# Four-piece GpSimd squares and low halves in chunks 0 and 1, ScalarE casts for half of w_out, and later joins for the last quarter-row of w_in

## The chip, the cores and the metric

One core of a Trainium2 chip runs the whole problem. The metric is the device time of one launch in microseconds, lower is better. TensorE (PE) multiplies, VectorE (DVE), ScalarE (ACT) and GpSimd (POOL) do the elementwise work, SyncE (SP) issues the DMAs. TensorE's clock has two levels, 1.2 and 2.4 GHz; the granted clock is shown as a share of the higher one.

## The reference, cut to what matters

```python
# attention, 8 batches, 8 heads, 512 local and 32 global tokens, head size 64
s_g = scale * q_g @ k_all^T              # global queries see all 544 keys
s_l = [scale * q_l @ k_g^T, scale * q_l @ k_l^T where |i - j| <= 32]
attn_out = concat(softmax(s_g) @ v_all, softmax(s_l) @ v_all)
# feed-forward on the 8 * 544 = 4352 tokens
x = attn_out as (8 * 544, 512)
h = x @ w_in                             # w_in 512 x 2048, in double precision
g = h * cos(h)
out = (g @ w_out).astype(float32)        # w_out 2048 x 512, in double precision
```

## The kernel before

**Numbers.** The two weights arrive as 64-bit doubles. ScalarE scales the upper word (`decode`, L231), VectorE shifts the lower word (L232) and joins the two into one float32 (L236, the "join"). A float32 is then carried as two float16 halves: a high half by a cast (`split_w`, L243) and a low half, value minus high half, by GpSimd (`pool_tt`, L217). x and g get the same split: `xh`/`xl` (L669 ScalarE, L670 VectorE) and `gh`/`gl` (L849 ScalarE, L850 GpSimd). Each product is three float16 matmuls: high by high, high by low, low by high.

**w_in** comes in eight pieces (row quarter kc = k // 2, column half k % 2): `w_in_load`, `w_in_max`, `w_in_piece`. Pieces 4 and 7 come as two halves of 512 columns (`raw_wi7_0`, `raw_wi7_1`). **w_out** comes in 16 pieces of 128 rows (`w_out_load`, `w_out_max`, `w_out_piece`); their largest values are reduced at L250 into `wos`, for pieces 8 to 15 from a first copy, `raw_wm8` to `raw_wm15`, which is loaded again later as `raw_wo8` to `raw_wo15` for the decoding.

**The stages.** Up to about 82 us the attention of batch 0 and w_in's preparation run. From there feed-forward chunks follow, two of 256 tokens per batch and one for the global tokens, each in eight steps j of two column blocks of h:

- `m1_a`: h into PSUM tile `ph_c_j` (L805, 24 matmuls of 256 columns; three buffers of `ph`)
- `m1_b`: `u` by ScalarE (L827) and VectorE (L828)
- `m1_c`: `w` = sine by ScalarE (L429)
- `m1_d`: the square of `w` on GpSimd (L843), `gf` on VectorE (L845, the last reader of `ph_c_j`, which frees its buffer), `gh` on ScalarE (L849), `gl` on GpSimd (L850)
- `m2_a`: two output tiles `po` (L865, 12 matmuls of 512 columns), which needs both w_out pieces 2j and 2j + 1

Beside chunks 0 and 1 run w_out's 16 pieces and the whole attention of batch 1 (scores `ps` L531, masked minimum `t` L549, exponentials L429, normalised `planes` L596/L597, DMA transposes `pt` L616, values `acc` L649, global queries `gacc` L741). Later chunks run beside the next batch's attention alone. `chunk_scales` prepares the chunk's constants `ca`, `cm`, `co`.

**Order.** Work is written down with `at(slot, phase, f, ...)`; `pr` gives the priority. A scheduler then places each engine's instructions, and a queue runs in that order: an instruction that waits holds everything behind it. `behind(ins, what)` orders an instruction after another one. The SP queue is one row too: a load that waits for its buffer holds the transposes behind it.

The few lines that matter most:

```python
WH = "DDDDDDDDDDDDDDDD"          # engine of w_out's 16 casts: all VectorE
SPLIT = 256                      # pool_tt: pieces of at most this many columns
decode(z, raw, wfs["s", kc], join_after="xs" if k >= 6 else "dx" if k >= 4 else None)
split_w(wo_h[:, j], wo_l[:, j], z, j % 4 < WLV, WH[j])
nc.gpsimd.tensor_tensor(w, w, w, op=ALU.mult)               # m1_d
nc.gpsimd.tensor_tensor(gl, gf, gh, op=ALU.subtract)        # m1_d
```

Of the kernel before, what the change touches and what calls it, by code (L numbers as in the profile page):

```python
# [15 lines left out]
ALU = mybir.AluOpType  # L16
# [30 lines left out]
SPLIT = 256  # L47
# [19 lines left out]
TPE = [1, 1, 1, 1]  # L67
TPV = [1, 0, 1, 0]
WLV = 0
MR = 2  # L70
SR = (1,)
AR = (1,)
WH = "DDDDDDDDDDDDDDDD"
DI = 3
QMA = 1
KQB = 3
# [15 lines left out]
W0 = -15  # L92
WE = -20
WM = 1
WL = [-22, -20, -17]
# [27 lines left out]
def body(tc, qf, v, wi, wo, mask, out):  # L123
    nc = tc.nc
# [4 lines left out]
    with ExitStack() as ctx:  # L129
# [11 lines left out]
        msk = cp.tile([P, MW], BF16, name="msk")  # L141
# [67 lines left out]
        def pool_tt(o, a, b, op, n=SPLIT):  # L209

            w = o.shape[-1]
            k = -(-w // n)
            while w % k:
                k += 1
            for i in range(k):
                c = slice(i * (w // k), (i + 1) * (w // k))
                nc.gpsimd.tensor_tensor(o[..., c], a[..., c], b[..., c], op=op)  # L217
# [21 lines left out]
            )  # L239
            behind(join.ins, join_after)  # L240

        def split_w(h, l, z, on_vector=False, cast="A"):
            {"A": nc.scalar.copy, "D": nc.vector.tensor_copy, "G": nc.gpsimd.tensor_copy}[cast](h, z)  # L243
            if on_vector:
                nc.vector.tensor_tensor(l, z, h, op=ALU.subtract)
            else:
                pool_tt(l, z, h, ALU.subtract)

        def raw_max(o, raw):
            return nc.vector.tensor_reduce(  # L250
# [28 lines left out]
        wfs = {}  # L279
# [45 lines left out]
        def w_in_piece(k):  # L325
            kc = k // 2
            parts = wfs.pop(("raw", k))
            n = 1024 // len(parts)
            for a, raw in enumerate(parts):
                c = slice(k % 2 * 1024 + a * n, k % 2 * 1024 + a * n + n)  # L330
                z = raw.bitcast(F32)[:, 1::2]
                decode(z, raw, wfs["s", kc], join_after="xs" if k >= 6 else "dx" if k >= 4 else None)
                split_w(wi_h[:, kc, c], wi_l[:, kc, c], z)

        wfi = cp.tile([P, 2], F32, name="wfi")
# [65 lines left out]
        def w_out_piece(j):  # L401
            if j < 8:
                raw = wo_raw[:, j]
            else:
                raw = w2.tile([P, 1024], U32, tag="raw", name=f"raw_wo{j}")
                nc.sync.dma_start(raw.bitcast(I64), wo[j * P : (j + 1) * P])
            z = w2.tile([P, DM], F32, tag="wy", name=f"z_wo{j}")
            decode(z, raw, wsc, low_after="wsc")
            split_w(wo_h[:, j], wo_l[:, j], z, j % 4 < WLV, WH[j])

        def w_out_done():
            m = ap_.tile([P, 1], F32, tag="wm", name="wm_o")
# [247 lines left out]
        def av_b(b, p):  # L660
            if p == 0:
                st["x", b] = (
                    ap_.tile([P, NPAIR, SL], F16, tag="xh", name=f"xh_{b}"),
                    ap_.tile([P, NPAIR, SL], F16, tag="xl", name=f"xl_{b}"),
                )
            xh, xl = st["x", b]
            acc = st.pop(("acc", b, p))
            sx = xs[:, p : p + 1]
            hi = nc.scalar.activation(xh[:, p], acc, AF.Identity, scale=sx)  # L669
            lo = nc.vector.scalar_tensor_tensor(  # L670
                xl[:, p], acc, sx, xh[:, p], op0=ALU.mult, op1=ALU.subtract
            )
            st["last_x", b, p] = (hi.ins, lo.ins)
            st["new_x"] = hi.ins


# [161 lines left out]
        def m1_d(c, j):  # L838
            w = st.pop(("u", c, j))[1]
            n = w.shape[-1]  # L840
            gh = mp.tile([P, n], F16, tag="gh", name=f"gh_{c}_{j}", bufs=4)
            gl = mp.tile([P, n], F16, tag="gl", name=f"gl_{c}_{j}", bufs=4)
            nc.gpsimd.tensor_tensor(w, w, w, op=ALU.mult)  # L843
            gf = gf_tile(c, j, n)
            nc.vector.scalar_tensor_tensor(  # L845
                gf, w, 0.5, st.pop(("ph", c, j)).rearrange("p a b -> p (a b)"),
                op0=ALU.subtract, op1=ALU.mult,
            )
            nc.scalar.copy(gh, gf)  # L849
            nc.gpsimd.tensor_tensor(gl, gf, gh, op=ALU.subtract)  # L850
            st["g2", c, j] = (gh, gl)

        def m2_a(c, j):
# [43 lines left out]
        def at(slot, phase, f, *a, pr=None):  # L897
            e = (phase, len(ev[slot]), f, a)
            ev[slot].append(e)
            pr = (slot, phase) if pr is None else pr if isinstance(pr, tuple) else (pr, phase)  # L900
            rank[slot, e[1]] = pr + (slot, e[1])
# [1 line left out]
        rank = {}  # L903

        def attn_pair(b, p, o):
            at(o["load"], PJ, load_qk, b, p)
            attn_rest(b, p, o)

        def attn_rest(b, p, o):
# [34 lines left out]
            )  # L944


        at(-24, PA, nc.sync.dma_start, msk, mask)
        for p in range(NPAIR):
            o = tight(U0 + SP0 * p, VD0 + SP0 * p)
            o["load"] = -23 if p < 2 else -22  # L950
            if p == 3:
                o["gd"], o["ge"] = -10, -9
            attn_pair(0, p, o)
        at(-23, PJ, load_v, 0)
        at(-19, PF, v_a, 0)
        at(-19, PG, v_b, 0)
        at(-19, PG2, v_c, 0)
        for k in range(8):
            if k < 4:
                at(WL[0] if k < 2 else WL[1], PJ, w_in_load, k)  # L960
            at(WE + k - WM, PH2, w_in_max, k, pr=W0 + k - WM)
            at(WE + k if k < 4 else -13 if k < 6 else -11, PK, w_in_piece, k, pr=(W0 + k, PJ))
            if k < 4:
                at(WE + k, PJ, w_in_load, k + 4, pr=W0 + k if k < 3 else W0 - 1)
        at(WE + 7 - WM, PI, w_in_max_done, pr=(W0 + 7 - WM, PH2))
# [125 lines left out]
```

## Time and profile before

| | |
|---|---|
| median of 3 runs | 959.17 us (958.49 to 959.61) |
| the profiled execution | 958.73 us, its span 956.9 us |
| PE busy | 904.6 us (95%) |
| ACT busy | 656.2 us (69%) |
| DVE busy | 587.8 us (61%) |
| POOL busy | 401.5 us (42%) |

The busy times are means over stages with different limits. Up to 82 us no matmul of the feed-forward can run; from 82 to about 206 us chunks 0 and 1 share the engines with w_out's preparation and batch 1's attention; from 206 us on the matmuls follow one another. A view by stretches shows which engine is full where, the waits show what ended PE's idle time, and groups of instructions by form show the price of one.

### The profile page before, as it was taken

The page shows a single profiled execution, that of the slowest core. Times are in us where ns is not written, and L with a number is a line of the kernel's source. Part 1 is how long each engine was busy: PE and PEld are TensorE (multiplying, and loading weights), DVE is VectorE, ACT ScalarE, POOL GpSimd, SP SyncE. Part 2 cuts the span into 40 slices and gives each one's busy share as a digit, 9 for nine tenths or more (in the row PEclk, how much of TensorE's full clock was granted, in tenths as well). Part 3 has the DMA queues.
Part 4 walks back from the last instruction along what each step waited for, and adds up shares of the span by engine and source line. Part 5 has one row for each costly group of instructions (what it writes and reads, how often), then busy time and mean ns, then how long its engine had stood idle before and what let it go on. Part 6 is the DMA issues. An engine that isn't in the chain of part 4 may idle for free.

```text
span 956.9 us, 19857 instructions
## 1 busy us (share of the span) xinstructions
PE 904.6 (95%) x7643; PEld 602.3 (63%) x7643; DVE 587.8 (61%) x1576; ACT 656.2 (69%) x1411; POOL 401.5 (42%) x412
## 2 busy tenths in 40 slices
PE   6657988999999999999999999999999999999995
PEld 4445665556666666666666666666666666666663
DVE  5998999856474757566665757564756555423231
ACT  6886599866777677776877777677777775443341
POOL 5856555432434343433334333324343434444441
PEclk8657899999999999999999999999999999999999
DMA  9936237535244453536262724352442433000000
GB/s 365 388 126 198 69 84 179 141 70 159 53 93 86 121 111 67 111 90 144 46 133 45 186 41 124 44 151 53 108 71 67 85 67 59 23 1 23 1 23 23
DMA packets 155176, 96.41 MB, mean 101 GB/s; under 512 B 141000, under 2 KB 141128, under 8 KB 153288
## 3 DMA queue, kind: packets, MB, share of 16 engines
q1 hardware_dynamic: 155080, 95.13, 39.7%
q8 instruction: 60, 0.98, 0.4%
q14 instruction: 36, 0.29, 0.1%
HBM read 51.59 MB, written 8.91 MB: 63 GB/s over the span
## 4 chain that ended last, share of the span: by engine, by line
PE 80%; DVE 9%; ACT 3%; DMA 3%; issue 2%; POOL 2%; SPq 0%; ACTq 0%; POOLq 0%; DVEq 0%
PE ph L805 35%; PE po L865 34%; PE ps L531 5%; PE acc L649 3%; DVE planes L597 2%; PE gps L686 1%; PE gacc L741 1%; DMA raw_wo<-wo 1%; DMA vr<-v 1%; ACT t L429 1%; DVE t L549 1%; DVE raw_wi L236 1%; DVE vl L516 1%; DVE z_wo L236 1%; DMA ptg<-planes_g 1%
## 5 line engine op out<-in xcount | busy, mean ns | idle before, releaser
L865 PE MATMUL po<-wo_hl,gh 128*128 128x512 f16 x1088 | 321.3, 380 | 0.7 <-POOL wo_hl L217 0.6
L805 PE MATMUL ph<-xh,wi_h 128*128 128x256 f16 x1024 | 282.3, 276 | 3.4 <-DVE gf L845 3.4
L805 PE MATMUL ph<-xl,wi_h 128*128 128x256 f16 x1024 | 281.3, 275 | 2.1 <-DVE xl L670 2.1
L805 PE MATMUL ph<-xh,wi_l 128*128 128x256 f16 x1024 | 281.3, 275 | 0.0
L850 POOL TENSOR_TENSOR gl<-gf,gh 128x512 f16<-128x512 f32 x136 | 163.5, 1203 | 237.1 <-ACT gh L849 237.0
L843 POOL TENSOR_TENSOR w<-w 128x512 f32<-128x512 f32 x136 | 143.9, 1058 | 258.5 <-ACT w L429 249.5
L805 PEld LDWEIGHTS <-wi_h 128*128 128x128 f16 x2176 | 207.1, 99 | 57.9 <-issue 22.2
L865 PE MATMUL po<-wo_hl,gl 128*128 128x512 f16 x544 | 201.3, 380 | 0.0
L865 PEld LDWEIGHTS <-gh 128*128 128x128 f16 x1088 | 106.7, 98 | 102.3 <-issue 1.1
L849 ACT CAST gh<-gf 128x512 f16<-128x512 f32 x136 | 83.1, 613 | 126.8 <-DVE gf L845 126.8
L828 DVE SCALAR_TENSOR_TENSOR u<-u,cm,ph 128x512 f32<-128x512 f32 x136 | 101.2, 744 | 99.5 <-ACT u L827 99.5
L429 ACT ACTIVATE w<-u,ca 128x512 f32<-128x512 f32 x136 | 97.9, 721 | 93.9 <-DVE u L828 91.9
L845 DVE SCALAR_TENSOR_TENSOR gf<-w,ph 128x512 f32<-128x512 f32 x136 | 93.0, 684 | 108.7 <-POOL w L843 107.9
L429 ACT ACTIVATE t<-t,mn 128x192 f32<-128x192 f32 (+1 forms) x256 | 116.7, 458 | 10.3 <-DVE mn L549 9.8
L805 PEld LDWEIGHTS <-wi_l 128*128 128x128 f16 x1088 | 107.2, 99 | 16.7 <-issue 3.4
L597 DVE SCALAR_TENSOR_TENSOR planes<-t,sm,planes 128x192 f16<-128x192 f32 (+1 forms) x232 | 104.9, 511 | 11.7 <-ACT planes L596 10.9
L827 ACT ACTIVATE u<-ph,cm 128x512 f32<-128x512 f32 x136 | 92.0, 678 | 21.9 <-PE ph L805 15.4
L865 PEld LDWEIGHTS <-gl 128*128 128x128 f16 x544 | 53.3, 98 | 64.5 <-issue 2.1
L549 DVE CUSTOM_DVE_ANT_0 t<-ps,msk 128x192 f32<-128x192 f32 (+1 forms) x256 | 82.9, 366 | 11.7 <-PE ps L531 10.8
L596 ACT ACTIVATE planes<-t,sm 128x192 f16<-128x192 f32 (+1 forms) x232 | 86.2, 455 | 2.4 <-DVE gsm L713 2.2
L531 PE MATMUL ps<-qkr 64*128 64x192 f32 (+1 forms) x496 | 78.0, 383 | 8.4 <-DMA qkr<-qf 5.5
L429 ACT ACT_TABLE_LOAD x58 | 74.4, 1283 | 3.6 <-DVE u L828 2.0
(148 smaller groups left out, 924.5 us busy)
## 6 DMA issues: line engine op xcount, KB each, us to landing
qkr<-qf SPq DMA_DIRECT2D x31, 608.0 KB, 5.0
vr<-v SPq DMA_DIRECT2D x8, 1280.0 KB, 6.4
out<-o SPq DMA_DIRECT2D x34, 256.0 KB, 2.0
raw_wi<-wi SPq DMA_DIRECT2D x6, 1024.0 KB, 12.2
wo_hl<-wo SPq DMA_DIRECT2D x8, 512.0 KB, 11.7
raw_wm<-wo SPq DMA_DIRECT2D x8, 512.0 KB, 4.3
raw_wo<-wo SPq DMA_DIRECT2D x8, 512.0 KB, 4.7
raw_wi<-wi SPq DMA_DIRECT2D x4, 512.0 KB, 12.4
```

The lines of the kernel that those rows point to most:

```text
L429: ins = nc.scalar.activation(*a, **k).ins
L531: nc.tensor.matmul(pt[h][:, c], q[r, QZ[j] : QZ[j] + P], k[r, z : z + w], start=True, stop=True, skip_group_check=True,)
L549: nc.vector.tensor_tensor_reduce(t[:, h], pt[h], msk[:, MOFF[i] : MOFF[i] + w], NAL, 3.0e38, ALU.add, ALU.min, mn[:, h : h + 1],)
L596: a = nc.scalar.activation(hi, t[:, h], AF.Identity, scale=r)
L597: d = nc.vector.scalar_tensor_tensor(lo, t[:, h], r, hi, op0=ALU.mult, op1=ALU.subtract)
L805: nc.tensor.matmul(ph[:, a], w[:, kc, f], x[:, kc, q], start=first and ip == 0, stop=last and ip == 2, skip_group_check=True,)
L827: nc.scalar.activation(u, ph, AF.Identity, bias=m)
L828: nc.vector.scalar_tensor_tensor(u, u, m, ph, op0=ALU.subtract, op1=ALU.subtract)
L843: nc.gpsimd.tensor_tensor(w, w, w, op=ALU.mult)
L845: nc.vector.scalar_tensor_tensor(gf, w, 0.5, st.pop(("ph", c, j)).rearrange("p a b -> p (a b)"), op0=ALU.subtract, op1=ALU.mult,)
L850: nc.gpsimd.tensor_tensor(gl, gf, gh, op=ALU.subtract)
L865: nc.tensor.matmul(po[k], g[:, a * CT + k * P : a * CT + (k + 1) * P], w[:, 2 * j + a], start=(j == 0 and i == 0), stop=(j == NS - 1 and i ...
```

## The change

Five things are edited.

1. The squares (L843) and `gl` (L850) of chunks 0 and 1 go through `pool_tt` in pieces of `PS` = 128 columns: four GpSimd instructions of 128 columns in place of one of 512, 32 times. Later chunks keep one.
2. `WH`: the casts of w_out's pieces 0 to 7 move from VectorE to ScalarE.
3. `J7`, `L7`: the two joins of w_in's piece 7 are ordered behind `xl` of batch 0's last pair ("xl3"), and the piece is written down at slot -5 in place of -11.
4. `SW` = 256 is named as the width of w_out's low-half pieces, the same as `SPLIT` was.
5. `LO` writes the first loads (mask, q and k of batch 0, v of batch 0, w_in's pieces 0 and 1) as one string. The SP queue's first 31 rows stay the same.

```diff
+SW = 256
+LO = "m01v2345"
+J7 = "xl3"
+L7 = -5
+PS = 128
-WH = "DDDDDDDDDDDDDDDD"
+WH = "AAAAAAAADDDDDDDD"
...
-        def split_w(h, l, z, on_vector=False, cast="A"):
+        def split_w(h, l, z, on_vector=False, cast="A", n=SPLIT):
...
-                pool_tt(l, z, h, ALU.subtract)
+                pool_tt(l, z, h, ALU.subtract, n)
...
-                decode(z, raw, wfs["s", kc], join_after="xs" if k >= 6 else "dx" if k >= 4 else None)
+                decode(z, raw, wfs["s", kc], join_after=J7 if k == 7 else "xs" if k == 6 else "dx" if k >= 4 else None)
...
-            split_w(wo_h[:, j], wo_l[:, j], z, j % 4 < WLV, WH[j])
+            split_w(wo_h[:, j], wo_l[:, j], z, j % 4 < WLV, WH[j], SW)
...
+            if (b, p) == (0, 3):
+                st["xh3"], st["xl3"] = hi.ins, lo.ins
...
-            nc.gpsimd.tensor_tensor(w, w, w, op=ALU.mult)
+            pool_tt(w, w, w, ALU.mult, PS if c < 2 else n)
...
-            nc.gpsimd.tensor_tensor(gl, gf, gh, op=ALU.subtract)
+            pool_tt(gl, gf, gh, ALU.subtract, PS if c < 2 else n)
...
-            at(WE + k if k < 4 else -13 if k < 6 else -11, PK, w_in_piece, k, pr=(W0 + k, PJ))
+            at(WE + k if k < 4 else -13 if k < 6 else -11 if k < 7 else L7, PK, w_in_piece, k, pr=(W0 + k, PJ))
```

The scheduler places the instructions of chunks 0 and 1 anew, on all engines. Three places show it. (Trailing numbers are buffer numbers; `wos` and `xl` are named above, `cm` and `ca` are chunk constants.)

VectorE, at the first `xl` of batch 0, before:

```order
L236 SCALAR_TENSOR_TENSOR raw_wi7_1_320<-raw_wi7_1_320 128x512
L196 TENSOR_SCALAR cm_0_1202<-ca_0_1201 128x1
L250 TENSOR_REDUCE wos_108<-raw_wm12_1008 128x1
L670 SCALAR_TENSOR_TENSOR xl_0_1039<-acc_0_0_548,xs_90,xh_0_1038 128x512
L670 SCALAR_TENSOR_TENSOR xl_0_1039<-acc_0_1_681,xs_90,xh_0_1038 128x512
L670 SCALAR_TENSOR_TENSOR xl_0_1039<-acc_0_2_797,xs_90,xh_0_1038 128x512
```

The same place now:

```order
L255 TENSOR_REDUCE wos_108<-raw_wm12_996 128x1
L675 SCALAR_TENSOR_TENSOR xl_0_1027<-acc_0_0_548,xs_90,xh_0_1026 128x512
L675 SCALAR_TENSOR_TENSOR xl_0_1027<-acc_0_1_681,xs_90,xh_0_1026 128x512
L675 SCALAR_TENSOR_TENSOR xl_0_1027<-acc_0_2_797,xs_90,xh_0_1026 128x512
L795 TENSOR_SCALAR cm_0_1202<-cm_0_1202 128x1
L255 TENSOR_REDUCE wos_108<-raw_wm13_999 128x1
L796 TENSOR_SCALAR ca_0_1201<-ca_0_1201 128x1
L675 SCALAR_TENSOR_TENSOR xl_0_1027<-acc_0_3_923,xs_90,xh_0_1026 128x512
L241 SCALAR_TENSOR_TENSOR raw_wi7_0_318<-raw_wi7_0_318 128x512
L241 SCALAR_TENSOR_TENSOR raw_wi7_1_320<-raw_wi7_1_320 128x512
```

Piece 7's two joins moved from ahead of the four `xl` to behind them.

VectorE, at the first `gf` (chunk 0, step 0; it frees the first `ph` buffer), before; the L232 rows are the shifts of w_out's pieces:

```order
L232 TENSOR_SCALAR wo_hl_88<-wo_hl_88 128x512 x2
L757 SCALAR_TENSOR_TENSOR xg_97<-gacc_0_0_1064,pvs_98,xg_97 128x2x32
L232 TENSOR_SCALAR wo_hl_88<-wo_hl_88 128x512
L420 TENSOR_SCALAR osc_96<-hsc_95,wr_o_1034 128x1
L232 TENSOR_SCALAR wo_hl_88<-wo_hl_88 128x512 x5
L232 TENSOR_SCALAR raw_wo8_1515<-raw_wo8_1515 128x512
L232 TENSOR_SCALAR raw_wo9_1524<-raw_wo9_1524 128x512
L845 SCALAR_TENSOR_TENSOR gf_0_0_1217<-w_0_0_1210,ph_0_0_1050 128x512
```

The same place now:

```order
L237 TENSOR_SCALAR wo_hl_88<-wo_hl_88 128x512
L279 TENSOR_SCALAR wr_o_1022<-wr_o_1022 128x1
L237 TENSOR_SCALAR wo_hl_88<-wo_hl_88 128x512
L835 SCALAR_TENSOR_TENSOR u_0_2_1290<-u_0_2_1290,cm_0_1202,ph_0_2_1265 128x512
L852 SCALAR_TENSOR_TENSOR gf_0_0_1220<-w_0_0_1210,ph_0_0_1038 128x512
L237 TENSOR_SCALAR wo_hl_88<-wo_hl_88 128x512
```

Of ten shifts ahead of that `gf` two are left, and one `u` now stands ahead of it.

ScalarE, from `gh` of chunk 0's step 0 on, before (`vh_1_0` is the first value tile of batch 1):

```order
L849 CAST gh_0_0_1214<-gf_0_0_1217 128x512
L849 CAST gh_0_1_1246<-gf_0_1_1249 128x512
L429 ACTIVATE w_0_2_1279<-u_0_2_1278,ca_0_1201 128x512
L827 ACTIVATE u_0_3_1333<-ph_0_3_1308,cm_0_1202 128x512
L429 ACTIVATE w_0_3_1334<-u_0_3_1333,ca_0_1201 128x512
L515 ACTIVATE vh_1_0_1225<-vr_1_1048,vs_1_1168 128x640
```

The same place now; `wo_hl_88<-z_wo0` is the cast of w_out's piece 0, which waits for VectorE's join of that piece:

```order
L856 CAST gh_0_0_1214<-gf_0_0_1220 128x512
L434 ACTIVATE w_0_2_1291<-u_0_2_1290,ca_0_1201 128x512
L834 ACTIVATE u_0_3_1351<-ph_0_3_1326,cm_0_1202 128x512
L248 CAST wo_hl_88<-z_wo0_1235 128x512
L248 CAST wo_hl_88<-z_wo1_1242 128x512
L856 CAST gh_0_1_1252<-gf_0_1_1258 128x512
L236 ACTIVATE z_wo2_1298<-wo_hl_88,wsc_109 128x512
L434 ACTIVATE w_0_3_1352<-u_0_3_1351,ca_0_1201 128x512
L236 ACTIVATE z_wo3_1305<-wo_hl_88,wsc_109 128x512
L856 CAST gh_0_2_1313<-gf_0_2_1319 128x512
L248 CAST wo_hl_88<-z_wo2_1298 128x512
```

The casts now stand in ScalarE's row between the steps of chunk 0. In SP's queue the loads of `raw_wo10` and `raw_wo11` moved from behind the eighth DMA transpose of batch 1 to behind the fourth, and those of pieces 12 and 13 from behind the eighth to behind the fourth too. On PE the third step of chunk 0 runs whole before the first `gacc`, and `ph_0_3` stands ahead of the second `gacc` and of batch 1's first scores, which followed the other way round.

## Rows read from the trace of the kernel before

**Rows 1.** Stretches: length, busy PE, PEld, DVE, ACT, POOL (counts), PEclk, DMA share, GB/s.
```profile
100.00:118.00 18.00, 18.00 (x138) 12.73 (x135) 15.67 (x42) 9.48 (x15) 10.47 (x10) 0.93 0.21 74
118.00:133.00 15.00, 11.37 (x76) 7.88 (x75) 14.80 (x31) 14.92 (x36) 9.16 (x12) 1.00 0.27 87
133.00:150.00 17.00, 16.50 (x131) 11.15 (x131) 15.64 (x45) 16.96 (x40) 7.63 (x8) 0.90 0.40 77
150.00:182.00 32.00, 27.57 (x215) 17.48 (x213) 28.78 (x82) 26.17 (x63) 16.76 (x20) 0.95 0.79 206
206.00:300.00 94.00, 94.00 (x841) 62.40 (x837) 59.31 (x164) 67.99 (x146) 35.45 (x32) 1.00 0.45 105
```

**Rows 2.** PE's waits, 66 to 206 us: us in total, times, longest.
```profile
PE ph L805 <- DVE gf L845: 3.4, 2, 3.2
...
PE gacc L741 <- DMA ptg<-planes_g: 3.1, 1, 3.1
PE ph L805 <- DVE xl L670: 2.1, 1, 2.1
```

**Rows 3.** The chain that ended last, three pieces: start, us, what.
```profile
90.57 5.50 DMA ptg<-planes_g
...
99.27 7.01 PE ph L805 x48
...
220.02 2.73 PE ph L805 x24
```

**Rows 4.** Timeline of DVE, SP and POOL, 70 to 97 us: start, us, instruction.
```profile
71.81 1.22 DVE L236 SCALAR_TENSOR_TENSOR raw_wi<-raw_wi 128x1024 uint32<-128x1024 uint32 x1
...
74.75 1.59 SPq L392 DMA_DIRECT2D raw_wm<-wo  x2
...
77.12 3.85 DVE L236 SCALAR_TENSOR_TENSOR raw_wi<-raw_wi 128x1024 uint32<-128x1024 uint32 x3
...
92.15 2.26 POOL L843 TENSOR_TENSOR w<-w 128x512 f32<-128x512 f32 x2 [6.26 <-ACT w L429]
...
96.63 0.68 DVE L845 SCALAR_TENSOR_TENSOR gf<-w,ph 128x512 f32<-128x512 f32 x1
```

**Rows 5.** DMA issues, page: count, KB each, median us to landing.
```profile
raw_wm<-wo SPq DMA_DIRECT2D x8, 512.0 KB, 4.3
```

**Rows 6.** DVE by form, casts 96 to 150, planes to 210 us: count, busy us, mean ns.
```profile
L243 DVE CAST wo_hl<-z_wo 128x512 f16<-128x512 f32 x8 | 5.4, 682 | 0.0
...
L597 DVE SCALAR_TENSOR_TENSOR planes<-t,sm,planes 128x224 f16<-128x224 f32 x16 | 11.9, 778 | 0.0
```

**Rows 7.** Line 597, 96 to 210 us: count, ns shortest/median/longest.
```profile
L597 DVE SCALAR_TENSOR_TENSOR planes<-t,sm,planes x33: 404/444/1369, 129.0 to 210.0; 128x192 f16<-128x192 f32 x17, 128x224 f16<-128x224 f32 x16
```

**Rows 8.** POOL by form, 96 to 210 us, last line from 0 to 85 us.
```profile
L850 POOL TENSOR_TENSOR gl<-gf,gh 128x512 f16<-128x512 f32 x15 | 19.3, 1292 | 20.2 <-ACT gh L849 20.1
L843 POOL TENSOR_TENSOR w<-w 128x512 f32<-128x512 f32 x14 | 16.3, 1168 | 19.1 <-ACT w L429 19.1
...
L513 POOL TENSOR_TENSOR vl<-vr,vh 128x128 f16<-128x128 f32 x4 | 1.7, 428 | 0.0
```

**Rows 9.** Timeline of DVE and POOL, 125 to 133 us.
```profile
125.41 1.16 POOL L850 TENSOR_TENSOR gl<-gf,gh 128x512 f16<-128x512 f32 x1 [3.51 <-ACT gh L849]
...
125.46 1.65 DVE L236 SCALAR_TENSOR_TENSOR z_wo<-z_wo,wo_hl 128x512 uint32<-128x512 uint32 x1
...
127.15 0.63 DVE L236 SCALAR_TENSOR_TENSOR z_wo<-z_wo,wo_hl 128x512 uint32<-128x512 uint32 x1
...
129.74 3.12 POOL L217 TENSOR_TENSOR wo_hl<-z_wo,wo_hl 128x256 f16<-128x256 f32 x4
...
130.73 1.60 DVE L597 SCALAR_TENSOR_TENSOR planes<-t,sm,planes 128x192 f16<-128x192 f32 x2
```

**Rows 10.** ACT by form, 96 to 210 us: count, busy us, mean ns of one.
```profile
L849 ACT CAST gh<-gf 128x512 f16<-128x512 f32 x15 | 8.9, 609 | 5.5 <-DVE gf L845 5.5
```

**Rows 11.** ACT's waits, 88 to 118 us: us in total, times, longest.
```profile
ACT gh L849 <- DVE gf L845: 5.5, 3, 2.8
```

More of the change, by code (lines that the diff above doesn't have):

```diff
@@ L905, in attn_pair @@
         def attn_pair(b, p, o):
-            at(o["load"], PJ, load_qk, b, p)
+            if b:
+                at(o["load"], PJ, load_qk, b, p)
             attn_rest(b, p, o)
@@ L944, in tight @@
             )
-        at(-24, PA, nc.sync.dma_start, msk, mask)
+        for i, e in enumerate(LO):
+            if e == "m":
+                at(-24, i, nc.sync.dma_start, msk, mask)
+            elif e == "v":
+                at(-24, i, load_v, 0)
+            elif e < "4":
+                at(-24, i, load_qk, 0, int(e))
+            else:
+                at(-24, i, w_in_load, int(e) - 4)
         for p in range(NPAIR):
@@ L953, in body @@
             attn_pair(0, p, o)
-        at(-23, PJ, load_v, 0)
         at(-19, PF, v_a, 0)
@@ L958, in body @@
         for k in range(8):
-            if k < 4:
-                at(WL[0] if k < 2 else WL[1], PJ, w_in_load, k)
+            if 2 <= k < 4:
+                at(WL[1], PJ, w_in_load, k)
             at(WE + k - WM, PH2, w_in_max, k, pr=W0 + k - WM)
-            at(WE + k if k < 4 else -13 if k < 6 else -11, PK, w_in_piece, k, pr=(W0 + k, PJ))
+            at(WE + k if k < 4 else -13 if k < 6 else -11 if k < 7 else L7, PK, w_in_piece, k, pr=(W0 + k, PJ))
             if k < 4:
```

## The prediction

> **What bounds the kernel now.** I read the busy times by stretches first, then PE's waits, then the timeline around each wait. From 206 us on PE has no idle time (94.00 of 94.00 us) at the full clock [rows 1], and the change leaves that work as it is. So the end moves with the moment at which PE has done chunks 0 and 1, and what can be won is what PE loses before. That loss has three parts. At 82 us PE waits 2.1 us for the first `xl` [rows 2]. In the nineties it waits 3.1 us for the transposed global planes, and after that the clock is granted at half: 48 matmuls of `ph` take 7.01 us where 24 take 2.73 later, so 7.01 - 2 x 2.73 = 1.6 us go to the clock [rows 3]. Between 118 and 182 us it idles 3.63 + 0.50 + 4.43 = 8.6 us, and the granted clock is 0.90 and 0.95 in two stretches, which at a lower level of half speed is 0.20 x 17 / 2 = 1.7 and 0.10 x 32 / 2 = 1.6 us of lost work [rows 1]. Together from 118 us on about 11.9 us. No engine is idle enough there to explain this alone: VectorE is at 14.80 of 15, 15.64 of 17 and 28.78 of 32 us, ScalarE is at 14.92 of 15 and 16.96 of 17 us from 118 to 150 us and then has 5.8 us left in 32 [rows 1]. So VectorE is nearly full all through, and ScalarE is full in the middle. Anything taken from VectorE counts outside the middle, anything given to ScalarE costs in it.
>
> **The change part by part.** *The first loads and the width SW* change nothing that runs: the queue's head and the pieces are the same. Zero.
>
> *The joins of w_in's piece 7.* Before, VectorE takes three joins in a row from 77.12 us, 3.85 us together, and then a `wos` reduction and the first `xl`, for which PE waits; one join of 1024 columns alone took 1.22 us [rows 4]. Two of the three go behind the `xl`, so up to 3.85 - 1.22 = 2.6 us leave the path. What is late next is the copy `raw_wm12`, which the `wos` ahead of the first `xl` reads: its load was issued at 74.75 us [rows 4] and a load of that kind lands after 4.3 us in the median [rows 5], so at 79.1, where that join would end at 77.12 + 1.22 = 78.3. That takes 0.8 us back at most: 1.8 to 2.6, and I take the middle, 2.2. The piece's columns are wanted by step 4 of chunk 0 only, some 20 us later; that hides the late joins and the low half behind them. If that cover were gone it would cost the two joins again.
>
> *The first gf.* Its square was done when the first of two GpSimd instructions from 92.15 us ended, about 93.2, but VectorE worked off ten shifts of w_out and took `gf` at 96.63 [rows 4]. Now two shifts and a `u` stand ahead. The next step of PE needs that `gf`'s buffer, but before it waited in the same place for the global planes anyway. The planes landed at 90.57 + 5.50 = 96.1 [rows 3] after a wait of 3.1 [rows 2], so PE was through its third step at 93.0; with 2.2 us off, at 90.8. The `u` of that step, by ScalarE and VectorE, and `gf` (0.68) [rows 4] follow: I count 2.4 us, an estimate from three such instructions of 0.68 and the steps between them. So PE idles 2.4 us where it idled 3.1, and the transposed planes, issued after the first `gacc`, now land beside step 3. Gain 0.7 us. The lower bound is 0, because the wait is only swapped; the upper is 3.1, if step 3 meets no wait. The half clock behind the gap stays, since the gap does.
>
> *The casts of pieces 0 to 7.* VectorE loses eight casts, 5.4 us [rows 6]. ScalarE gets eight at the 0.609 us of `gh`, the same shape [rows 10]: 4.9 us. Four of them fall before 118 us, where ScalarE works 9.48 of 18 us and PE is busy all the time [rows 1], so neither side counts directly. The other four fall into the full middle: 4 x 0.61 = 2.4 us on the path there, if nothing else slips.
>
> *The GpSimd pieces.* No square or `gl` of 128 columns is in the trace; the nearest row is a subtraction of 128 columns at 0.428 us [rows 8]. Four take 1.71 us against 1.17 for a square and 1.29 for a `gl` [rows 8]: 16 x 0.54 + 16 x 0.42 = 15.4 us more on GpSimd, which is busy 9.16 of 15 us in its fullest stretch [rows 1]. What it buys is on VectorE. A join that met a whole `gl` took 1.65 us, the next one, alone, 0.63 [rows 9]: VectorE stood for 1.0 us. The 16 `planes` instructions of 224 columns take 778 ns in the mean [rows 6] where the median of all of line 597 is 444 [rows 7]: 16 x 0.33 = 5.3 us lost. If a piece of a quarter of the length holds VectorE half as long on the whole, some 3 us come back on these and perhaps as much again on the joins and values. But pieces do not let a row of such instructions through: beside four GpSimd pieces of 256 columns two `planes` took 1.60 us, 0.80 each against the shortest of 0.404 [rows 9, 7]. Four quarters can cost four short stands in place of one long one, 4 x 0.2 = 0.8 against 0.9. So between 6 us back and, because GpSimd is busy 15 us longer, 3 us lost; I take 1, near the row of the alternation, since `planes` come eight in a row.
>
> The Trainium skill's page "SBUF — State Buffer", section "Who interferes with whom", says that VectorE and GpSimd share one port pair as an exclusive lock, held for a whole instruction, when the VectorE instruction has two SBUF inputs or runs in a two-port mode, and that issue order decides who blocks. The stretched join agrees with it [rows 9]. By that rule a lone instruction would stand for at most a quarter of what it stands now, the 6 us would be nearer, and the sum 10.9 us in place of 5.9; the alternating rows speak for 1.
>
> *What moves with it.* The loads of w_out's pieces 10 to 13 no longer stand behind the fifth to eighth transposes. PE's gaps from 150 to 182 us, 4.4 us and 1.6 of clock [rows 1], lie where those pieces arrive. With VectorE's relief I count half of them, 3.0 us. In the middle I count the casts' 2.4 us, less half of the 2.7 us that the same four casts cost VectorE: -1.0.
>
> Sum: 2.2 + 0.7 + 1.0 + 3.0 - 1.0 = 5.9 us. From the profiled execution's 958.73 us that is 952.8; the median of the runs lies 0.44 above it, so **953.3 us**. The ends of the terms together give 3.6 us slower (1.8 + 0 - 3 + 0 - 2.4) and 21 us faster (2.6 + 3.1 + 6 + 6.0 + 3.6); the rivals below say when either way is taken.
>
> **The rivals.** *PE closes its gaps.* If VectorE was what PE waited for everywhere, its 5.4 us of casts and up to 6 us of standing cover nearly the whole loss from 118 us on. Then 2.9 us of start and 11 of 11.9 us come back: 958.7 - 13.9 = 944.8, in the median 945. For it speaks VectorE's load in all stretches; against it that ScalarE is just as full from 118 to 150 us and takes the casts.
>
> *ScalarE takes over (slower).* The new casts stand in its row and wait for VectorE's joins, with `gh`, `w` and the next scaling behind them. A wait of ScalarE's `gh` for VectorE was 5.5 us in 3 [rows 11], 1.8 each. One such hold for each of four pairs is 7.3 us, with 4.9 us of casts 12.2. Of the 8.5 us that ScalarE has free between 100 and 118 us [rows 1] half, 4.3, takes some of it up, and the start gives 2.9: 958.7 + 12.2 - 4.3 - 2.9 = 963.7, in the median 964. It turns slower from the point where holds and casts exceed what is absorbed and the lead, 7.2 us. For it speaks that ScalarE has 0.1 us free from 118 to 150 us [rows 1]; against it that the casts come early, where it is half idle, and that each join is now ahead of less work.
>
> *The lead is lost.* The start is 2.9 us earlier but the middle, ScalarE-bound, ends at the same time, and GpSimd's pieces give VectorE nothing. Then 958.7, in the median 959. Nothing moves after 150 us because PE has its backlog of `po` to work off in any case.
>
> **How the numbers follow.** A measurement of this kernel can tell about 0.2% from no change, 1.9 us. I give the forecast (950 to 957) 0.50, PE closing its gaps 0.17, the lost lead 0.15, ScalarE taking over 0.18. Faster: 0.50 + 0.17 = 0.67; same 0.15; slower 0.18. For the range I leave out half of the closed gaps and a little under half of ScalarE's case, 0.08 on either side: 945 to 963.
>
> **What the profile after would show.** Right: PE's wait for the first `xl` gone or under 0.4 us; `ph` of step 3 starting near 93 to 94 us in place of 99.27 [rows 3]; line 243 on VectorE at eight, and eight casts of about 0.61 us on ScalarE; squares and `gl` at about 0.4 us a piece; `planes` at a mean under 0.778; the start of PE's unbroken stretch before 182 us. Wrong: ScalarE waiting on VectorE joins between 95 and 135 us (its row takes over); pieces well over 0.43 us, with `planes` no shorter (no relief); PE's gaps between 150 and 182 us as large as before. The prediction falls if PE's idle time from 118 to 182 us is not smaller than 8.6 us, or if the start is not earlier.

## The result and the profile after

The changed kernel takes 949.74 us in the median (949.26 to 950.59, 5 runs); the kernel before, on the same chip, 959.17 (956.93 to 959.85). The ratio is 0.9906, with a 95% interval of 0.9892 to 0.9920: 9 us faster, where 5.9 were forecast. A second set of runs gave 950.44 us and 0.9909 [0.9892, 0.9926]. One measurement of a ratio is thus good to about 1.5 us, a difference of two to about 2 us. Below, "x us against before" is one minus the ratio, times 959, always with the runs of before on the same chip.

The stretches after the change, as in [rows 1] (length, busy PE, PEld, DVE, ACT, POOL with counts, granted clock, DMA share, GB/s):

```profile
100.00:118.00 18.00, 15.81 (x118) 9.81 (x117) 15.88 (x38) 14.72 (x31) 17.98 (x32) 1.00 0.26 88
118.00:133.00 15.00, 13.54 (x99) 9.72 (x97) 13.88 (x36) 13.98 (x29) 9.11 (x19) 1.00 0.56 116
133.00:150.00 17.00, 12.70 (x101) 7.63 (x100) 14.44 (x42) 16.97 (x41) 13.22 (x25) 0.90 0.58 174
150.00:182.00 32.00, 30.01 (x256) 18.28 (x254) 27.50 (x80) 29.02 (x71) 19.98 (x39) 1.00 0.60 149
206.00:300.00 94.00, 94.00 (x814) 62.40 (x812) 56.47 (x159) 68.86 (x154) 35.97 (x32) 1.00 0.44 98
```

PE still has no idle time from 206 us on, so all of the gain lies before. GpSimd is now full from 100 to 118 us (17.98 of 18, before 10.47). And from 118 to 182 us PE idles 1.46 + 4.30 + 1.99 = 7.75 us, against 8.6 before: hardly less. In the second trace of the same kernel it is 1.46 + 4.98 + 2.43 = 8.87 us:

```profile
118.00:133.00 15.00, 13.54 (x100) 9.85 (x98) 13.90 (x38) 13.96 (x29) 9.34 (x20) 1.00 0.57 117
133.00:150.00 17.00, 12.02 (x98) 7.21 (x97) 14.09 (x41) 16.95 (x41) 13.19 (x25) 0.90 0.57 166
150.00:182.00 32.00, 29.57 (x254) 18.18 (x252) 27.00 (x78) 28.21 (x70) 19.63 (x37) 1.00 0.61 150
```

**By its own criterion the prediction stands in one trace and falls in the other.** From 150 to 182 us the idle time did halve (4.43 to 1.99 and 2.43 us). From 133 to 150 us it grew (0.50 to 4.30 and 4.98), and from 100 to 118 us there is some where there was none (2.19 us). Taken together, the gaps did not close.

PE's waits from 66 to 206 us, as in [rows 2]:

```profile
PE po L872 <- POOL wo_hl L222: 9.7, 6, 2.6
PE ph L812 <- DVE gf L852: 3.3, 3, 2.2
PE tr L616 <- DVE pt L619: 3.2, 1, 3.2
PE acc L654 <- ACT pt L619: 2.2, 1, 2.2
...
PE ph L812 <- DVE xl L675: 0.5, 1, 0.5
...
PE gacc L748 <- DMA ptg<-planes_g: 0.2, 1, 0.2
```

The wait for the first `xl` is down from 2.1 to 0.5 us, that for the transposed global planes from 3.1 to 0.2. In their place stands another: six times, 9.7 us in all (before twice, 0.6 us), `po` waits for the low half of a piece of w_out, GpSimd's work.

**Where the 9 us are.** I cut both traces at two places that mean the same work: the first product with `xl`, and the 205th product with w_out (`po`). From there to PE's end it is 711.38 us in both. Between the two, one row each of before, after, and the second trace of after (columns as above):

```profile
82.33:235.98 153.65, 141.75 (x1194) 93.86 (x1194) 125.25 (x318) 111.97 (x246) 72.36 (x76) 0.94 0.49 127
```
```profile
80.32:226.51 146.19, 132.90 (x1194) 88.77 (x1194) 118.42 (x314) 119.55 (x259) 95.28 (x174) 0.98 0.52 134
```
```profile
79.04:227.06 148.02, 133.44 (x1195) 89.20 (x1195) 118.64 (x315) 119.67 (x260) 96.15 (x174) 0.97 0.52 132
```

The same 1194 matmuls keep PE busy for 8.9 us less. Idle time is 11.90 before and 13.29 and 14.58 after; with the start, 82.33 + 11.90 = 94.23 before against 93.61 and 93.62: a gain of 0.6 us. (The start itself moves by 1.3 us between the two traces of one kernel, and the idle time makes up for it.) The rest is in two parts. Before, the clock was granted at half in four stretches between the cuts:

```profile
78.75:85.58 6.83, 4.59 (x29) 3.23 (x29) 6.70 (x13) 3.02 (x5) 6.83 (x10) 0.50 0.41 118
95.82:102.65 6.83, 6.54 (x62) 4.78 (x62) 6.83 (x16) 1.96 (x3) 4.30 (x4) 0.50 0.01 2
133.37:136.78 3.41, 3.41 (x18) 2.45 (x17) 3.41 (x9) 3.40 (x11) 1.74 (x2) 0.50 0.62 118
177.74:181.15 3.41, 3.10 (x21) 1.24 (x16) 2.18 (x6) 3.39 (x10) 1.15 (x3) 0.50 0.27 103
```

After, in two (in the second trace in three):

```profile
92.13:95.54 3.41, 3.41 (x19) 2.36 (x17) 3.41 (x8) 0.61 (x1) 3.35 (x7) 0.50 1.09 206
146.74:150.16 3.42, 3.42 (x9) 1.22 (x8) 3.42 (x14) 3.40 (x7) 1.17 (x3) 0.50 0.80 153
```

PE's time in them, 16.3 us before and 6.8 after (8.5 in the second trace), counts half as lost: 8.15 against 3.41 (4.25), a gain of 4.7 (3.9) us. What is left is PE's work at full clock, 133.6 against 129.5 (129.2), 4.1 (4.4) us, and nearly all of it is one group, the score matmuls `ps`. Before and after, between the two cuts:

```profile
L531 PE MATMUL ps<-qkr 64*128 64x224 f32 (+1 forms) x96 | 19.5, 372 | 2.3 <-DVE mn L549 2.1 <-DVE gmn L699 0.2
```
```profile
L536 PE MATMUL ps<-qkr 64*128 64x192 f32 (+1 forms) x96 | 14.3, 362 | 0.0
```

As many matmuls, each about as long, in 5.2 us less: they overlap more (part of that is clock). The trace has two records for each of the four score matmuls of a group, and the counts here are of records. PE's timeline shows how they overlap. Before, four in a row of one head, and after a short wait four of the other; after, eight in a row in which the heads take turns:

```profile
117.36 0.97 PE L531 MATMUL ps<-qkr 64*128 64x192 f32 x4
118.51 0.97 PE L531 MATMUL ps<-qkr 64*128 64x192 f32 x4 [0.18 <-DVE gmn L699]
```
```profile
100.68 0.98 PE L536 MATMUL ps<-qkr 64*128 64x192 f32 x8
```

Two heads lie in rows 0 to 63 and 64 to 127 of one tile; in turns, eight cost what four cost. The Trainium skill's page "TensorE: Matmul & The Clock Gate", section "Part 3: Packing small matmuls — row/col tiling", says that matmuls on different row groups of the array run at the same time; the rows agree, 0.98 us for eight against 0.97 for four. The scheduler, which makes each engine's order, had put 9 of the 24 groups of batches 0 to 2 in turns before, and 14 after. None of the edits touches those lines.

So there were two readings. **Theory A**, the prediction's: VectorE, let go by GpSimd's pieces and freed of joins, is what PE waits for. **Theory B**, read off this bookkeeping: start, clock and paired scores; the pieces themselves only cost.

### The profile page after: what moved, and what is told of

It is laid out like the page before. It is cut to its first block, busy times and chain, and to the rows that moved or that the text cites. A ratio compares the mean times of both kernels' runs of the same rounds, so it can differ in the third digit from the quotient of the medians.

```text
span 947.5 us, 19962 instructions
## 1 busy us (share of the span) xinstructions
PE 896.2 (95%) x7643; PEld 597.5 (63%) x7643; DVE 578.5 (61%) x1568; ACT 660.6 (70%) x1419; POOL 421.9 (45%) x508
## 4 chain that ended last, share of the span: by engine, by line
PE 82%; DVE 7%; ACT 3%; POOL 3%; DMA 2%; issue 1%; SPq 0%; ACTq 0%; POOLq 0%
PE ph L812 36%; PE po L872 35%; PE ps L536 5%; PE acc L654 4%; PE gps L693 2%; DVE planes L602 1%; PE gacc L748 1%; DMA raw_wo<-wo 1%; DMA vr<-v 1%; ACT t L434 1%; POOL wo_hl L222 1%; POOL vl L518 1%; DVE z_wo L241 1%; POOL wi_l L222 1%; DVE raw_wi L241 1%
## 5 line engine op out<-in xcount | busy, mean ns | idle before, releaser
L222 POOL TENSOR_TENSOR gl<-gf,gh 128x512 f16<-128x512 f32 (+1 forms) x184 | 173.8, 955 | 230.2 <-ACT gh L856 229.3
L222 POOL TENSOR_TENSOR w<-w 128x512 f32<-128x512 f32 (+1 forms) x184 | 152.9, 841 | 248.3 <-ACT w L434 236.0
L602 DVE SCALAR_TENSOR_TENSOR planes<-t,sm,planes 128x192 f16<-128x192 f32 (+1 forms) x232 | 100.4, 493 | 13.9 <-ACT planes L601 13.2
L554 DVE CUSTOM_DVE_ANT_0 t<-ps,msk 128x192 f32<-128x192 f32 (+1 forms) x256 | 82.8, 366 | 11.4 <-PE ps L536 10.4
L536 PE MATMUL ps<-qkr 64*128 64x192 f32 (+1 forms) x496 | 73.0, 382 | 6.1 <-DMA qkr<-qf 5.4
```

Of the source, the lines that this page charges most:

```text
L536: nc.tensor.matmul(pt[h][:, c], q[r, QZ[j] : QZ[j] + P], k[r, z : z + w], start=True, stop=True, skip_group_check=True,)
L554: nc.vector.tensor_tensor_reduce(t[:, h], pt[h], msk[:, MOFF[i] : MOFF[i] + w], NAL, 3.0e38, ALU.add, ALU.min, mn[:, h : h + 1],)
L602: d = nc.vector.scalar_tensor_tensor(lo, t[:, h], r, hi, op0=ALU.mult, op1=ALU.subtract)
```

## The experiments

**One part undone at a time.** First the pieces:

```
-PS = 128
+PS = 512
```

> The changed kernel with GpSimd's squares and gl of chunks 0 and 1 whole again (512 columns); joins and casts stay changed. Theory A (the prediction's: the pieces let VectorE go and so close TensorE's gaps): the pieces' 1.0 us and the 3.0 us that were to follow from them come back, 949.7 + 4.0 = 953.7 us, and TensorE's idle time from 118 to 182 us is back at 8.6 us or more. Theory B (read from the two traces: the gain is an earlier start of 2.0 us, 4.7 us less lost to half clock, 4.1 us less of score matmuls because more of their groups take the two heads in turn, less 1.4 us of more idle; the pieces themselves cost, since w_out's low halves wait behind them on GpSimd): TensorE's waits for wo_hl from GpSimd fall from 9.7 us to under 3 us; 13 of the 24 groups of batches 0 to 2 take the heads in turn instead of 14, which is +0.9 us; 943 to 950 us.

Measured: 955.28 us, ratio 0.9955 [0.9942, 0.9969], 4.3 us against before. The pieces are worth 4.7 us, with the joins and casts there, as theory A had it (4.0), and PE's idle time from 118 to 182 us is up at 11.3 us. Theory B's 943 to 950 is out. The wait for w_out's low halves is 6.6 us in 5 without the pieces, so most of it doesn't come from them; that it comes from `po` being further ahead is likely, not shown.

```
-WH = "AAAAAAAADDDDDDDD"
+WH = "DDDDDDDDDDDDDDDD"
```

> The changed kernel with all sixteen casts of w_out by VectorE again; pieces and joins stay changed. Theory A: the casts were put at a cost of 1.0 us, so 949.7 - 1.0 = 948.7 us, VectorE having room for 5.4 us more from 118 to 150 us. Theory B: the start, the clock and TensorE's waits for wo_hl (9.7 us) stay as in the changed kernel; 13 groups take the heads in turn instead of 14, +0.9 us: 950.6 us. A rival (C: VectorE is what sets the pace from 100 to 150 us, and the casts were its relief): 5.4 us of casts come back on VectorE and TensorE's waits for VectorE grow by 3 us or more: 953 us or more.

Measured: 950.24 us, 0.9899 [0.9886, 0.9911]. Within the error the same as with the casts: the ratio is 0.7 us better, the time 0.5 us worse, so a cost of 1.0 us, as forecast, can't be told from none. Rival C's 953 or more is out. Its sign did come: PE's waits for `gf` grew from 3.3 to 7.3 us. Those for w_out's low halves fell from 9.7 to 4.9 us at the same time: one wait took the place of another.

```
-J7 = "xl3"
-L7 = -5
+J7 = "xs"
+L7 = -11
```

> The changed kernel with the joins of w_in's last piece back where they were, ahead of the last xl; pieces and casts stay changed. Theory A: the joins' 2.2 us and the earlier gf's 0.7 us come back: 952.6 us, with the gaps from 118 to 182 us as in the changed kernel. Theory B: the first product with xl starts 2.0 us later again, after an idle time of 2.1 us, and the granted clock is at half around 82 us as before; 11 of 24 groups take the heads in turn instead of 14 (+2.6 us): 949.7 + 2.0 + 4.7 + 2.6 = 959.0 us if all of the clock's gain is due to the joins, 954.3 us if none is.

Measured: 959.70 us, 1.0000 [0.9988, 1.0011]. Without the joins' move the other two parts bring nothing that can be told from zero, although VectorE is busy 115.67 us between the cuts where it was 125.25, a fall of 9.6 us of which the casts are 5.4. The joins are worth 9 us here where their terms were 2.2 and 0.7, so A's 952.6 is out; B had the size, from 954.3 to 959.0. PE's waits from 82 to 206 us show a single long one for w_out, and in its stretch PE works 9.87 of 17 us at a mean clock of 0.80:

```profile
PE po L872 <- POOL wo_hl L222: 6.8, 2, 6.5
PE gacc L748 <- DMA ptg<-planes_g: 3.1, 1, 3.1
PE po L872 <- DVE o L881: 2.7, 1, 2.7
PE ph L812 <- DVE xl L675: 2.7, 1, 2.7
```
```profile
133.00:150.00 17.00, 9.87 (x58) 5.83 (x56) 14.85 (x39) 16.94 (x40) 13.54 (x25) 0.80 0.66 156
```

**The joins alone**: the changed kernel with `PS = 512` and all sixteen casts on VectorE, which is the kernel before with the joins moved:

> The kernel before with one part of the change alone: the joins of w_in's last piece behind the last xl. Theory A (prediction): -2.2 and -0.7 us, 959.0 - 2.9 = 956.1 us. Theory B (start, clock, order): the first product with xl starts 2.0 to 3.1 us earlier (80.3 us in the changed kernel, 79.3 us without the pieces, 82.3 us before), and the half clock at that place is one unit of 3.4 us or none instead of two, which gives back 1.7 to 3.4 us: 959.0 - 3.7 to 6.5 = 952.5 to 955.3 us.

Measured: 958.16 us, 0.9986 [0.9975, 0.9997], 1.3 us. Both theories gave more, 956.1 and 952.5 to 955.3 us. The first product with `xl` starts at 80.62 us, so the lead is there, and it is lost again in a new place, PE's `acc` behind the transposed planes of batch 1:

```profile
PE acc L654 <- DMA pt<-planes: 8.3, 3, 4.1
PE gps L693 <- DVE mn L554: 3.6, 2, 2.3
PE gacc L748 <- DMA ptg<-planes_g: 2.7, 1, 2.7
```

This comes out as the third rival, the lost lead, at 958 where it had 959. Joins alone 1.3, joins and casts 4.3, pieces and casts 0.0, joins and pieces 9.7, all three 9.0 us: **the parts don't add up**. The casts, nothing beside the pieces, bring 3.0 us without them (error 1.7). Each of these kernels has its own order, so that could lie in the edits or in the orders; the pieces alone and the casts alone were not run.

**The heads in turns.** If B's pairing is a gain in itself, more of it must bring more. First by chaining the matmuls of a group (batches 0 to 2), the rest left to the scheduler:

```
 def sc_a(b, p, i):
...
-nc.tensor.matmul(pt[h][:, c], ...)
+mm = nc.tensor.matmul(pt[h][:, c], ...).ins
+if b < 3 and last is not None:
+    tc.add_manual_dep(mm, last.name, order, reason="heads_in_turn")
+last = mm
```

> The changed kernel with one thing added: the four score matmuls of a group of batches 0 to 2 are chained so that the two heads (rows 0 to 63 and 64 to 127) take turns in TensorE's queue, where in 10 of the 24 groups the two of one head stood together. Nothing that is computed changes. Theory A: TensorE's own work is as it was and the gaps decide: 949.7 us, within 0.2%. Theory B: a group in turns took 0.91 us and one not in turns 1.79 us; 4 of the 10 lie behind 82 us, where TensorE is the bound, so -3.5 us: 946.2 us; if the 6 of batch 0 count too, -8.8 us: 940.9 us. Score matmuls between 80 and 227 us fall from 13.4 us to about 10 us.

Measured: 954.20 us, 0.9945 [0.9931, 0.9959]: 3.5 to 3.7 us slower than the changed kernel, where A had no change and B a gain. Between the cuts `ps` is no shorter (16.1 us against 14.3), the start is at 82.13 us again and the global planes are waited for 5.4 us. Chaining batch 0 changed the order ahead of the start, so the same for batches 1 and 2 alone (`0 < b < 3`):

> The changed kernel with the score matmuls of batches 1 and 2 alone chained to take the two heads in turn; batch 0 is left as it is, because with it chained the start was 1.8 us later and the transposed globals were waited for 5.4 us. Theory B (a group in turns 0.91 us, one not in turns 1.79 us): 4 groups more in turns, -3.5 us: 946.2 us, with the start at 80.3 us. Theory D (which order the scheduler makes of it decides, the pairing is small beside that): anywhere from 946 to 954 us, and the sum of score matmuls falls by 2 us or more while idle time or half clock grows by as much.

Measured: 950.23 us, 0.9895 [0.9879, 0.9911]. The same as the changed kernel. PE's work at full clock falls by only 0.3 to 0.6 us, and start and idle time together grow by 1.7. B's 946.2 is out.

**The order held.** An edit can make the scheduler deal out a new order on all engines, so an undone edit may undo more than itself. For the next runs I recorded each engine's queue from a built kernel and chained it, instruction by instruction (the edit in short; `by` holds the kernel's instructions by engine):

```
+for e, queue in HELD.items():
+    for a, b in zip(queue, queue[1:]):
+        tc.add_manual_dep(by[e][b], by[e][a].name, order, reason="held_order")
```

In the order of the changed kernel, with `PS = 512`:

> The changed kernel with the squares and gl of chunks 0 and 1 whole (512 columns) as in the run without pieces, but every engine's queue held in the order of the changed kernel (each whole operation where its first piece stood), so that nothing is moved and only the pieces are undone. Theory A (the pieces let VectorE in between, so the gain is in how the two engines share): the whole operations cost the 5.5 us that they cost when the order was free, 955 us, and VectorE's long stretches behind GpSimd are back. Theory D (the gain of the pieces was the other order that the scheduler made when it was told of pieces): 949.7 us within 1.5, or faster by up to 3 us, since GpSimd has 4 x 0.43 = 1.7 us instead of 1.17 us for each square or gl with the pieces and TensorE waits behind it for wo_hl.

Measured: 953.66 us, 0.9932 [0.9915, 0.9948]. The reverse, in the order of the run without pieces, with `PS = 128`:

> The run without pieces (joins and casts changed, 955.3 us), with every engine's queue held in that run's order, and the pieces of 128 columns put in, four in a row where the whole operation stood. Theory A: the pieces give their gain in any order: 955.3 - 5.5 = 949.8 us. Theory D: the order decides, so 955.3 us, or slower by up to 3 us for the longer GpSimd work.

Measured: 956.31 us, 0.9953 [0.9937, 0.9970]. So in one order the pieces bring 2.2 to 2.5 us, in the other nothing; and the order, with whole operations, brings 2.2 (0.9955 to 0.9932), each with an error of about 2. Of the pieces' 4.7 us about half is each, as far as that goes. Neither A nor D alone holds. No run holds an order with nothing else changed, so what the chaining costs between the cuts is not measured. From the 205th `po` to PE's end, where the queues are chained too, both runs take the same 711.38 us as the free ones. A cost of the chaining would make the pieces' gain smaller in the first order and larger in the second. A size between, in the changed kernel's order, `PS = 256`:

> The changed kernel with the squares and gl of chunks 0 and 1 in two pieces of 256 columns instead of four of 128, every queue held in the order of the changed kernel. Theory A (short pieces let VectorE in): between the whole operations in this order (ratio 0.9932) and the four pieces (0.9906), so 0.992, 951 us. Theory E (GpSimd's sum is what TensorE waits for, 9.7 us for wo_hl): two pieces at the 0.66 us of w_out's low halves of 256 columns are 1.32 us where four are 1.71, 32 x 0.39 = 12 us less on GpSimd, and the waits for wo_hl fall to under 7 us: 947 to 949 us.

Measured: 951.55 us, 0.9917 [0.9902, 0.9932], between the two, as A had it. E's 947 to 949 is out, and the wait for w_out's low halves fell to 8.4 us, not to under 7. The stretch between the cuts for 512 and 256 columns, in that one order:

```profile
78.97:231.18 152.21, 136.78 (x1194) 89.96 (x1194) 123.98 (x312) 118.29 (x257) 73.49 (x78) 0.96 0.49 128
```
```profile
79.00:228.45 149.45, 135.01 (x1194) 89.37 (x1194) 120.72 (x313) 119.14 (x259) 81.86 (x110) 0.97 0.51 131
```

With 128 columns these are the two rows of the changed kernel above. The same instructions keep VectorE busy 123.98, 120.72 and 118.4 to 118.6 us; length and gain against before follow step by step: 152.2, 149.5, 146.2 to 148.0, and 6.5, 8.0, 8.7 to 9.0 us. The steps in the gain are each within the error; from one end to the other it is about as large as its error. In the order of the run without pieces (first row whole, second in pieces) VectorE's busy time fell as well, from 123.75 to 117.65 us, and the time did not:

```profile
79.27:233.98 154.71, 138.93 (x1195) 90.43 (x1194) 123.75 (x312) 118.22 (x257) 73.99 (x78) 0.95 0.49 126
```
```profile
80.21:232.43 152.22, 136.64 (x1195) 90.18 (x1194) 117.65 (x313) 118.92 (x259) 95.97 (x174) 0.97 0.50 128
```

The profiled execution of the run without pieces was its slowest, 956.93 us, so these two lengths differ by more than the medians do. The relief is there in both orders, and whether it pays seems to hang on the order.

Last the pairs, with everything else where it stood. In the changed kernel's order five groups of batches 1 and 2 are put four in a row with the heads in turn, at the place of their second half:

> The changed kernel, every queue held in its order, except that in batches 1 and 2 the five groups of score matmuls that were not four in a row with the heads in turn are put so, at the place of their second half. Theory B (pairing counts): 4 x 0.88 us = 3.5 us less work of TensorE after 82 us: 946.2 us. Theory F (between 100 and 180 us TensorE is not the bound: w_out's rows, by VectorE, ScalarE and GpSimd, are; what TensorE saves there comes back as idle time): the work falls by 3.5 us and idle time grows by about as much, 949.7 us within 1.0.

Measured: 951.59 us, 0.9923 [0.9904, 0.9943]. PE's work falls by 1.4 to 1.7 us, start and idle time together grow by 4.2:

```profile
78.98:229.01 150.03, 131.19 (x1195) 86.71 (x1195) 116.83 (x310) 117.77 (x256) 95.37 (x174) 0.98 0.50 130
```

No gain, and B's 946.2 is out. That fits F, by which what TensorE saves comes back as idle time; here more came back than was saved. And in the order of the kernel before, ten groups:

> The kernel before, every queue held in its order, except that in batches 1 and 2 the ten groups of score matmuls that were not four in a row with the heads in turn are put so, at the place of their second half. None of the change's three parts is in it. Theory B: 4.1 us of the change's gain were this alone; 9 groups x 0.88 us = 7.9 us less work, 7.9 us at most: 951 to 955 us. Theory F: the work of TensorE falls by 6 to 8 us and idle time grows by as much: 959.2 us within 1.5, or up to 961 us because the scores of one head come later to VectorE.

Measured: 965.51 us (nine runs, 961.41 to 967.06), 1.0053 [1.0033, 1.0072]: 5 us slower than before, outside of what either theory gave. `ps` does shrink between the cuts, to less than in the changed kernel:

```profile
L531 PE MATMUL ps<-qkr 64*128 64x192 f32 (+1 forms) x96 | 13.5, 368 | 4.1 <-DVE mn L549 2.8 <-DVE gmn L699 1.4
```
```profile
81.07:242.67 161.60, 139.44 (x1195) 91.60 (x1194) 123.66 (x318) 112.20 (x246) 70.92 (x76) 0.92 0.46 121
```

PE idles 22.2 us instead of 11.9, and the mean clock is 0.92. The first head's scores come later than before, and its waits from 82 to 206 us grow where VectorE is the releaser: `ph` for `gf` 7.1 us in six, where [rows 2] has 3.4 in two. That VectorE gets the first head's scores too late is the likely reason; no run holds it apart from the others. What is shown is that the work PE saves, 5.8 us, is not saved at the end.

The changed kernel once more, unmodified, for the second trace and the spread used above:

> The changed kernel itself once more, for a second trace of it and for a comparison on the chip of the three runs beside it. All theories: 949.7 us, ratio to the kernel before 0.9906. What the second trace tells is how far the terms (start at 80.3 us, idle 13.3 us, 3.4 us lost to half clock, TensorE's own work 129.5 us between the first product with xl and the 205th of the products with w_out) move from one execution to the next with the order unchanged: in the two held orders the start moved by 0.9 and 1.4 us.

No run was measurably faster than the changed kernel; without the casts, or with batches 1 and 2 in turns, it is the same.

## Why the prediction was right, and where it was not

The time, 949.74, lies in the range, just under the 950 to 957 that were given the most weight, and the sign is right. In part that is luck: about 4 of the 9 us show as paired scores, for which the sum had nothing, and the sum had no term for what the new order would do as a whole. Of the steps:

**The joins, 2.2 us at the start: right in place, and about right in size.** PE's wait for the first `xl` went from 2.1 to 0.5 and 0.2 us in the two traces, the start from 82.33 to 80.32 and 79.04. VectorE's timeline after has one join where [rows 4] has three:

```profile
77.27 1.69 DVE L241 SCALAR_TENSOR_TENSOR raw_wi<-raw_wi 128x1024 uint32<-128x1024 uint32 x1
...
78.94 0.67 DVE L255 TENSOR_REDUCE wos<-raw_wm 128x1 f32<-128x512 f32 x1
79.53 2.05 DVE L675 SCALAR_TENSOR_TENSOR xl<-acc,xs,xh 128x512 f16<-128x512 f32 x3
...
82.88 1.28 DVE L241 SCALAR_TENSOR_TENSOR raw_wi<-raw_wi 128x512 uint32<-128x512 uint32 x2
84.08 0.67 DVE L255 TENSOR_REDUCE wos<-raw_wm 128x1 f32<-128x512 f32 x1
85.68 0.69 DVE L255 TENSOR_REDUCE wos<-raw_wm 128x1 f32<-128x512 f32 x1 [0.93 <-DMA raw_wm<-wo]
...
90.79 0.67 DVE L852 SCALAR_TENSOR_TENSOR gf<-w,ph 128x512 f32<-128x512 f32 x1
```

**The first gf, 0.7 us: the mechanism was right, a second one was missed.** `gf` comes at 90.79 where it came at 96.63 [rows 4], and PE idles 2.18 us for it where it idled 3.07 for the planes, as forecast (2.4 for 3.1). What I did not see: the last copy for w_out's scale is issued earlier too, at 82.3 us in place of 84.2 (VectorE takes it at 85.68; before it waited 2.15 us for it, until 87.94), and the `u` and sine behind it move with it. And "the half clock behind the gap stays" was wrong: behind the shorter gap it lasts 3.41 us, not 6.83, which gives 1.7 us back.

**The casts, -1.0 us: measured -0.7 in the ratio, with an error of about 2, so neither shown nor refuted.** ScalarE's waits from 84 to 206 us show no hold on a cast of w_out. It is at 13.98 of 15 us from 118 to 133 us, not full, and at 16.97 of 17 from 133 to 150, as before. The slower rival had these holds as its mechanism; it did not come up. The 3.6 us that the casts' term has at the fast end of the sum are worked out nowhere.

**The pieces, +1.0, and what moves with them, +3.0: 4.7 us together, the sum about right, the relief behind the 1.0 wrong.** GpSimd by form from 96 to 210 us, and line 602 on VectorE as in [rows 7]:

```profile
L222 POOL TENSOR_TENSOR gl<-gf,gh 128x128 f16<-128x128 f32 x60 | 29.5, 521 | 14.0 <-ACT gh L856 13.2 <-PE po L872 0.7
...
L222 POOL TENSOR_TENSOR w<-w 128x128 f32<-128x128 f32 x54 | 23.2, 458 | 14.8 <-ACT w L434 14.8
```
```profile
L602 DVE SCALAR_TENSOR_TENSOR planes<-t,sm,planes x40: 401/472/882, 123.3 to 204.0; 128x192 f16<-128x192 f32 x20, 128x224 f16<-128x224 f32 x20
```

A piece takes 0.46 to 0.52 us in the mean, a little over the 0.428 taken, and the longest `planes` fell from 1369 to 882 ns. VectorE's relief is 123.98 - 118.5 = 5.5 us of busy time in one order and 6.1 in the other, near the forecast's upper end of 6, not near 1. The row of alternating instructions [rows 9] by which I took 1 was the wrong one to be near. By the rule of the Trainium skill's page "SBUF — State Buffer", section "Who interferes with whom", which the prediction weighed, the sum would have been 10.9 us; the relief speaks for that rule, but the whole relief does not reach the end: 2.2 to 2.5 us in one order, none in the other. With errors of about 2 us that is not against 1.0 for the pieces and 3.0 for what moves. That the earlier loads of pieces 10 to 13 did their share of the 3.0, no run shows: none moved them alone.

**The step that failed: that PE's idle time from 118 to 182 us shrinks as its gaps from 150 to 182 us close, and that terms add up.** The gaps from 150 to 182 us did halve, and the clock there went from 0.95 to 1.00, as forecast. But the idle time came back from 133 to 150 us, and from 118 to 182 us it went from 8.6 to 7.75 and 8.87 us. `po` ran ahead by some 20 us in the middle and then waited for w_out's rows, six times. Nor does this idle time tell a kernel's time: it is 4.5 us in the run with the heads in turns in batches 0 to 2, which is slower than the changed kernel, and 10.4 us in the run without the casts, which is as fast. The gain shows up as clock granted (4.7 and 3.9 us), of which the sum had half of 1.6, and as PE's work, nearly all paired scores (4.1 and 4.4), of which it had none. Whether these are causes is another matter. Pairs alone are none: with batches 1 and 2 in turns, and in both held orders, PE lost in waits what they saved. Nor do the edits have values of their own: 2.2 + 0.7 for the joins was 1.3 alone and 9 with the pieces and casts.

**What stays open.** Why joins and pieces pay only together, and whether a place in the order is behind it; and why the freed VectorE shows as clock rather than as closed gaps. Between 76 and 182 us PE had five gaps of over 2 us before (2.02, 2.15, 3.07, 3.16, 2.06) and three after (2.22, 2.18, 2.59), and behind two of these three the clock was at half. That would fit shorter waits as the cause of the better clock. But before the change the clock was at half behind a gap of 1.61 us (at 175.0 us) and not behind the one of 2.06 (at 152.1), and with whole operations in the held order it was so from 174.91 us, behind one of 1.01 us (at 171.05). No run tested it by itself.

## What to carry to other kernels

Where a scheduler deals out the order, an edit is worth what it and the order it brings are worth together: undo it once freely and once with every queue held, before a cost is put on it. Time that an engine saves counts only where nothing else takes it up; cut the trace at two places of equal work and read start, idle time, clock and work apart, but don't take these parts for causes until a run has moved one alone. GpSimd's operations in short pieces let VectorE work beside them, at the price of GpSimd's own time (95.28 us busy between the cuts where it was 72.36), and that is worth trying where VectorE's instructions are stretched and GpSimd has room.

## What the runs showed of the hardware

Score matmuls of two heads on different halves of the rows cost half as much in turns: eight records in 0.98 us, where four of one head took 0.97. A piece of 128 columns on GpSimd cost 0.46 us (square) and 0.52 us (difference) in the mean, 1.8 and 2.1 us for four, where the whole took 1.18 and 1.29 us in the run with the order held. VectorE's busy time for the same instructions, in one order of the queues, was 124.0, 120.7 and 118.5 us beside GpSimd operations of 512, 256 and 128 columns. And the first product with `xl` started 1.3 us apart in two executions of one kernel, of which nothing was left at the 205th `po` (0.6 us, the other way).
